# The second product of a fused attention and MLP kernel with its operands exchanged

## The chip, the cores and the metric

The kernel runs on one core of a Trainium2 chip. The metric is the device time in microseconds of one execution. TensorE multiplies matrices (its weight loads are listed as PEld), VectorE (DVE) and ScalarE (ACT) move and transform tiles, GpSimd (POOL) does elementwise work and issues DMAs, and SyncE (SP) issues DMAs.

## The reference

```python
B, N, m, C = 4, 12480, 32, 128          # x: (B, N, C), inducing: (m, C)

def mab(q, kv):                          # one attention head, no projections
    s = (q @ kv.transpose(0, 2, 1)) / sqrt(C)
    a = exp(s - s.max(-1)); a /= a.sum(-1) + 1e-09
    return a @ kv

h = mab(I, x)                            # 32 inducing points attend to the tokens
y = mab(x, h).reshape(B * N, C)          # the tokens attend to the 32 results

hid = y @ w_in                           # (49920, 128) @ (128, 2048)
g = maximum(hid, 0) + alpha * minimum(hid, 0)
out = g @ w_out                          # (49920, 2048) @ (2048, 128), float32
```

## The kernel before

A batch of 12480 tokens is 6 super-tiles of 2048 tokens (`SUP`) and a rest of 192. A super-tile is 4 groups of 512 tokens (`GRP`), so a batch has 25 groups: 24 of 512 tokens and one of 192.

The second attention is never formed by itself. Per super-tile, `b_scores` multiplies the tokens with `hT` (the 32 results of the first attention) and ScalarE takes the exponentials into `e2`, with 4 groups stacked in the 128 partitions, 32 each. SyncE writes `e2` to DRAM (L371) and `b_rep` reads it back into `rep` (L379), in which the 32 rows of a group stand four times. `b_den` sums the exponentials by a product with `pick`; the reciprocals `rd` are kept and applied at the very end, since everything in between is linear under a positive factor: alpha * h + (1 - alpha) * max(h, 0) splits the activation into a linear part (`linear`, with `hA`) and a ReLU part whose weight `W1` holds w_out times (1 - alpha).

The work of a group is cut into 4 fills (2 for the rest of 192 tokens), 392 fills in all. One fill is

- in `fill`: 4 products side by side in 4 row groups of 32 (`hW` stationary, `rep` moving, 512 columns), each into one of 6 rotating PSUM banks (`ring`), the 4 evacuated with ReLU to bfloat16 tiles `gt` by ScalarE (L448) or VectorE (L450);
- in `mm2`, one fill later: the second product, 16 matmuls of 128x128. A block of 128 tokens of `gt` is stationary and 128 columns of `W1` move. They add up in one of two PSUM tiles `accs`, with tokens in the partitions and channels in the columns.

When a group's last `mm2` is issued, it is put into `held`, and the next fill's `flush` calls `finish`: VectorE multiplies the 128x512 accumulator by the reciprocals into `ob` (L503), and GpSimd issues one store of 256 KB (L516) in rows of 2 KB. The last four stores go by SyncE, and the very last evacuation is shared by VectorE and ScalarE.

Which engine evacuates which bank, and where `flush` stands, comes from `make_plan`, a beam search over assumed costs of each fill; it is written out before the program is built. All other work (loads of the next batch from GpSimd's queue at L129, DMA transposes `xT` at L143 and `e1T` at L273 from SyncE's queue, scores, denominators) is put into slots of fills by `at(slot, task, j, cost)`. `pin` fixes the program order of each engine and each DMA queue to the order in the source. While a batch runs, the first attention of the next batch is computed in groups 0 to 17 or so; the last batch has no such work beside it.

Of the kernel before, what the change touches and what calls it, by code (L numbers as in the profile page):

```python
# [9 lines left out]
EXP = mybir.ActivationFunctionType.Exp  # L10
# [6 lines left out]
P = 128  # L17
# [8 lines left out]
def kernel(  # L26
# [30 lines left out]
    def pin(bi):  # L57
# [17 lines left out]
    xt_pool = ctx.enter_context(tc.tile_pool(name="xtp", bufs=2))  # L75
    gt_pool = ctx.enter_context(tc.tile_pool(name="gtp", bufs=4))
    head_pool = ctx.enter_context(tc.tile_pool(name="headp", bufs=3))
    rep_pool = ctx.enter_context(tc.tile_pool(name="repp", bufs=3))
    dram = ctx.enter_context(
        tc.tile_pool(name="e2d", bufs=3, space=bass.MemoryType.DRAM)  # L80
    )
    ob_pool = ctx.enter_context(tc.tile_pool(name="obp", bufs=3))
    psum = ctx.enter_context(
        tc.tile_pool(name="ps", bufs=1, space=bass.MemoryType.PSUM)
    )
    ring = [psum.tile([P, GRP], f32, name=f"ring{i}") for i in range(RING)]
    accs = [psum.tile([P, NB, C], f32, name=f"acc{i}") for i in range(2)]
    ring_n = [0]

    def bank():  # L90
# [4 lines left out]
    def mm(o, lhsT, rhs, start=True, stop=True, **kw):  # L95
        return pin(nc.tensor.matmul(o, lhsT, rhs, start=start, stop=stop, **kw))  # L96
# [5 lines left out]
    def new_batch(b):  # L102
        st = Batch()
        st.b = b
        st.xT = xt_pool.tile([C, NS, NQ, GRP], bf16, name="xT", tag="xT")
        st.xTr = xt_pool.tile([C, JR, PR], bf16, name="xTr", tag="xTr")
        st.xn = {}
        st.e1T = {}
        st.sc = scale
        st.rs = None  # L110
        st.e2 = {}
        st.d = {}
        st.rep = {}
        st.rden = {}
        if b > 0:
            st.es = work.tile([P, NS + 1], f32, name="es", tag="es")
            st.hacc = work.tile([P, C], f32, name="hacc", tag="hacc")
            nc.vector.memset(st.es[:], 0.0)
            nc.vector.memset(st.hacc[:], 0.0)
        return st  # L120
# [101 lines left out]
    def warm(st, n=1):  # L222
        for _ in range(n):
            mm(
                accs[0][:, 1:, :].rearrange("p k c -> p (k c)"), ident[:],
                st.xT[:, 0, 0, : 3 * P], start=False, stop=False, skip_group_check=True,
            )

# [123 lines left out]
        evac_h(st, st.hA[:], pa[:, :C])  # L352


    def b_scores(st, s):
        ps = bank()
        if s < NS:
            for q in range(NQ):
                mm(ps[32 * q : 32 * q + 32, :], st.hT, st.xT[:, s, q, :])
            e2 = work.tile([P, GRP], bf16, name="e2", tag="e2")  # L360
            pin(nc.scalar.activation(out=e2[:], in_=ps[:], func=EXP, scale=scale_of(st)))  # L361
            w = GRP
        else:
            mm(ps[0:M, :REM], st.hT, st.xTr[:].rearrange("c j p -> c (j p)"))
            e2 = work.tile([M, REM], bf16, name="e2r", tag="e2r")
            pin(nc.scalar.activation(out=e2[:], in_=ps[0:M, :REM], func=EXP, scale=scale_of(st, M)))
            w = REM

        nq = NQ if s < NS else 1
        st.d[s] = dram.tile([32 * nq, w], bf16, name="e2d", tag="e2d" if s < NS else "e2dr")  # L370
        pin(nc.sync.dma_start(out=st.d[s][:], in_=e2[:]))  # L371
        st.e2[s] = e2
# [11 lines left out]
    def b_scores_pe(st, q):  # L384
        if q == 0:
            st.rep0 = rep_pool.tile([P, NQ, GRP], bf16, name="rep", tag="rep")
        ps = bank()
        mm(ps[:], st.hT4[:], st.xT[:, 0, q, :])
        pin(nc.scalar.activation(
            out=st.rep0[:, q, :], in_=ps[:], func=EXP, scale=scale_of(st)  # L390
        ))
        st.rep[q] = st.rep0[:, q, :]

    def b_den(st, s):
        e2 = st.e2.pop(s)
        ps = bank()
        if s < NS:
            for j in range(NB):
                mm(ps[:, j * NQ : (j + 1) * NQ], e2[:, j * P : (j + 1) * P], pick[:])
            rd = work.tile([P, NB, NQ], f32, name="rd", tag="rd")  # L400
            pin(nc.vector.reciprocal(
                out=rd[:].rearrange("p j q -> p (j q)"), in_=ps[:, : NB * NQ]
            ))
        else:
            for j in range(JR):
                mm(ps[:PR, j : j + 1], e2[:, j * PR : (j + 1) * PR], pick[0:M, 0:1])
            rd = work.tile([PR, JR, 1], f32, name="rdr", tag="rdr")
            pin(nc.vector.reciprocal(
                out=rd[:].rearrange("p j q -> p (j q)"), in_=ps[:PR, :JR]
            ))  # L410
        st.rden[s] = rd

    def shape_of(g):
        return (P, NB, 1) if g < NS * NQ else (PR, JR, 2)

    held = []

    def flush():  # L420
        while held:
# [31 lines left out]

    def mm2(st, g, j, gt):
        pp, nb, cp = shape_of(g)
        acc = accs[(st.b * NG + g) % 2]
        begun = (g % 2 == 1 and st.b + g > 1) or cp > 1
        for r in range(4):
            for i in range(cp):
                c = r * NJ + j * cp + i  # L460
                for k in range(nb):
                    k0 = (i * nb + k) * pp
                    mm(
                        acc[:pp, k, :], gt[:, r, k0 : k0 + pp], W1[:, c, :],
                        start=(j == 0 and r == 0 and i == 0 and k == 0 and not begun),
                        stop=False, skip_group_check=True,
                    )
        if j == NJ // cp - 1 and st.b * NG + g > 0:
            held.append((st, g))

# [6 lines left out]
        return []  # L477

    def linear(st, groups):
        for k in range(NB):  # L480
            for r, g in enumerate(groups):
                pp, nb, cp = shape_of(g)
                if k < nb:
                    mm(
                        accs[(st.b * NG + g) % 2][:pp, k, :],
                        st.rep[g][32 * r : 32 * r + 32, k * pp : (k + 1) * pp],
                        st.hA[32 * r : 32 * r + 32, :],
                        start=((r == 1 or cp > 1) and k == 0), stop=False, skip_group_check=True,
                    )

    def finish(st, g):
        pp, nb, _ = shape_of(g)
        acc = accs[(st.b * NG + g) % 2]
        s, q = divmod(g, NQ)
        rd = st.rden[s]
        rq = rd[:, :, q : q + 1]
        final = (st.b, g) == (B - 1, NG - 1)
        cut = nb - 1 if final else nb
        rbc = bass.AP(
            tensor=rq.tensor, offset=rq.offset, ap=[rq.ap[0], [rq.ap[1][0], cut], [0, C]]  # L500
        )
        ob = ob_pool.tile([P, NB, C], f32, name="ob", tag="ob")
        pin(nc.vector.tensor_tensor(  # L503
            out=ob[:pp, :cut, :], in0=acc[:pp, :cut, :], in1=rbc, op=MULT
        ))
        if final:
            pin(nc.scalar.activation(  # L507
                out=ob[:pp, cut, :], in_=acc[:pp, cut, :], func=COPY, scale=rd[:pp, cut, 0:1]
            ))
        t0 = st.b * N + s * SUP  # L510
        if s < NS:
            dst = out[t0 : t0 + SUP, :].rearrange("(p q j) c -> q p j c", q=NQ, j=nb)[q]
        else:
            dst = out[t0 : t0 + REM, :].rearrange("(p j) c -> p j c", j=nb)
        ending = st.b == B - 1 and g >= NG - 4
        pin((nc.sync if ending else nc.gpsimd).dma_start(out=dst, in_=ob[:pp, :nb, :]))  # L516
        st.rep.pop(g)


# [93 lines left out]
    pin(nc.scalar.copy(out=xn0[:, 2:4, :], in_=xs[:, 2:4, :]))  # L613
    st.xn[0] = xn0

    pool = accs[0][:, 0, :M]
    den = accs[1][:, 0, 0:1]
# [43 lines left out]
    at(0, lambda: warm(st, 2), 0)  # L661
    at(0, lambda: b_scores_pe(st, 1), 1, (240, "A", 480))
    at(0, lambda: b_den(st, 0), 2, (130, "D", 250))
    at(1, w_amat, 2, (950, "D", 250))
    at(1, lambda: h_linear(st), 3, (80, "D", 250))
    at(2, late_finish, 0)
# [2 lines left out]
    for b in range(B):  # L669
        base = b * NG  # L670
        for s in range(1, NS + 1):
            g = base + s * NQ - 4
            at(g, lambda b=b, s=s: b_scores(states[b], s), 3, (320, "A", 490))
            at(g + 1, lambda b=b, s=s: b_rep(states[b], s), 3)
            at(g + 2, lambda b=b, s=s: b_den(states[b], s), 3, (130, "D", 250))
        if b + 1 < B:
            n = b + 1

# [16 lines left out]
            at(k + 2, lambda n=n: h_linear(states[n]), 3, (80, "D", 250))  # L695
            at(k + 3, lambda n=n: b_rep(states[n], 0), 0)
            at(k + 3, lambda n=n: b_den(states[n], 0), 1, (130, "D", 250))

# [76 lines left out]
    for b, g, j in fills:  # L775
        gt = fill(states[b], g, j)
        for fn, _ in tasks.pop((b * NG + g, j), []):
            fn()
        if prev is not None:
            mm2(*prev)  # L780
        prev = (states[b], g, j, gt)
    mm2(*prev)
    flush()
    assert not tasks, tasks


# [28 lines left out]
```

## Time and profile before

| What | Value |
|---|---|
| median of 3 runs | 592.72 us (592.19 to 592.80) |
| profiled execution, span from its first to its last instruction | 591.0 us |
| TensorE busy, weight loads busy | 578.7 us, 434.2 us |
| VectorE busy, ScalarE busy, GpSimd busy | 517.7 us, 502.5 us, 84.9 us |
| `mm2`: matmuls of 128x128 | 6272, mean record 220 ns |
| `fill`: matmuls with 512 columns | 1536, mean record 385 ns |
| evacuation of 128x512 by ScalarE, by VectorE | 875 x 602 ns, 661 x 687 ns |
| `ob` of 128x512 on VectorE | 96 x 681 ns |
| stores from GpSimd's queue, 256 KB each | 93, landing in 2.9 us (median) |

The profile gives the span as its only time of the profiled execution; the median of the runs is 1.7 us above it. "Busy" is the time in which an engine has an instruction in work. Matmuls are pipelined: their records overlap, so the number of them times the mean is more than the busy time. "A x16" in the chain or the timeline stands for 16 instructions of one kind in a row. DMA shares are a mean over the core's 16 DMA engines.

### The profile page before, as it was taken

To read this page: it belongs to the slowest core of one execution; us is meant where nothing else is said; L and a number is where in the kernel's file an instruction comes from. 1 tells how busy PE (TensorE), PEld (TensorE's weight loads), DVE (VectorE), ACT (ScalarE), POOL (GpSimd) and SP (SyncE) were. 2 spreads that over 40 slices of the span, in tenths; PEclk is the share of its full clock that TensorE was granted. 3 is DMA by queue.
4 is the path that set the end of the run, shared out by engine and by line. 5 is a ranking of instruction groups with operands and counts; after the bars stand their busy time and mean duration, and the time that the engine had idled before them with its cause. 6 is when DMAs were issued, how large, how long until landed. Compare 5 with 4: busy or idle time off the path is not lost.

```text
span 591.0 us, 21769 instructions
## 1 busy us (share of the span) xinstructions
PE 578.7 (98%) x9218; PEld 434.2 (73%) x9219; DVE 517.7 (88%) x869; ACT 502.5 (85%) x988; POOL 84.9 (14%) x170
## 2 busy tenths in 40 slices
PE   5999999999999999999999999999999999999997
PEld 4677777777777777777777777777777777777776
DVE  3688998999889989998989899988988998998996
ACT  2579888888889988888888998888888988989987
POOL 6631111101011111110111111101101101101100
PEclk9999999999999999999999999999999999999999
DMA  9973978751237569953126597985122221221211
GB/s 198 210 174 90 177 149 163 154 140 55 86 87 165 125 128 185 171 137 92 60 83 142 121 163 129 185 159 131 59 70 80 89 93 54 92 91 56 94 47 62
DMA packets 81825, 70.10 MB, mean 119 GB/s; under 512 B 55440, under 2 KB 71072, under 8 KB 81728
## 3 DMA queue, kind: packets, MB, share of 16 engines
q0 software_dynamic: 12528, 38.51, 26.0%
q1 hardware_dynamic: 69056, 29.68, 25.0%
q8 instruction: 72, 1.18, 0.8%
q10 hardware_dynamic: 144, 0.52, 0.2%
q14 instruction: 25, 0.20, 0.1%
HBM read 40.20 MB, written 28.75 MB: 117 GB/s over the span
## 4 chain that ended last, share of the span: by engine, by line
PE 97%; DVE 1%; DMA 1%; ACT 1%; issue 0%; SPq 0%
PE acc L96 68%; PE ring L96 27%; PE ring L172 1%; DMA ind_f<-in_inducing_dram 1%; ACT gt L448 0%; DVE xT L178 0%; DVE gt L450 0%; DVE ob L503 0%; DVE xn L612 0%; ACT xT L180 0%; SPq L526 0%; ACT ob L507 0%; DVE hT L246 0%; DVE ind_b L562 0%; PE ring L565 0%
## 5 line engine op out<-in xcount | busy, mean ns | idle before, releaser
L448 ACT ACTIVATE gt<-ring 128x512 bf16<-128x512 f32 x899 | 469.5, 599 | 67.8 <-ACT gt L448 27.4
L450 DVE TENSOR_SCALAR gt<-ring 128x512 bf16<-128x512 f32 x669 | 435.1, 685 | 52.2 <-PE ring L96 37.8
L96 PE MATMUL acc<-W,gt 128*128 128x128 bf16 x6272 | 417.9, 220 | 0.2 <-DVE ob L503 0.2
L96 PEld LDWEIGHTS <-gt 128*128 128x128 bf16 x6272 | 352.4, 98 | 79.6 <-issue 76.8
L96 PE MATMUL ring<-rep,hW 32*128 32x512 bf16 (+1 forms) x1600 | 157.3, 379 | 0.0
L516 POOL DMA_DIRECT2D out_dram<-ob x96 | 51.8, 540 | 476.5 <-DVE ob L503 412.6
L96 PEld LDWEIGHTS <-hW 32*128 32x128 bf16 x1600 | 41.1, 91 | 41.6 <-issue 0.5
L503 DVE TENSOR_TENSOR ob<-acc,rd 128x512 f32<-128x512 f32 x96 | 65.4, 681 | 2.5 <-PE acc L96 2.5
L96 PE MATMUL acc<-hA,rep 32*128 32x128 bf16 x392 | 19.8, 214 | 0.0
L96 PEld LDWEIGHTS <-rep 32*128 32x128 bf16 x392 | 15.6, 93 | 5.6
L129 POOL DMA_DIRECT2D xn<-in_x_dram x28 | 15.3, 551 | 3.3 <-DMA xn<-in_x_dram 2.4
L197 ACT ACTIVATE e1t<-ring 128x256 bf16<-128x256 f32 (+1 forms) x13 | 4.8, 371 | 10.5 <-PE ring L96 10.4
L178 DVE COPY xT<-ring 128x1024 bf16<-128x1024 bf16 (+1 forms) x12 | 8.0, 669 | 5.2 <-PE ring L172 4.8
L361 ACT ACTIVATE e<-ring 128x512 bf16<-128x512 f32 x18 | 11.0, 612 | 0.0
L269 ACT ACTIVATE e<-ring 128x512 bf16<-128x512 f32 x18 | 10.9, 605 | 0.0
L96 PE MATMUL ring<-xT,hT 128*32 128x512 bf16 (+1 forms) x97 | 10.0, 389 | 0.0
L172 PE MATMUL ring<-ident,xn 128*128 128x128 bf16 x96 | 8.8, 249 | 0.9 <-DVE xn L612 0.9
L172 PEld LDWEIGHTS <-xn 128*128 128x128 bf16 x96 | 6.8, 112 | 1.0 <-DVE xn L612 1.0
L96 PEld LDWEIGHTS <-hT 128*32 128x32 bf16 (+1 forms) x122 | 3.7, 92 | 5.1 <-issue 2.6
L96 PE MATMUL ring<-xn,e1T 128*32 128x128 bf16 x288 | 7.4, 221 | 0.0
L96 PE MATMUL ring<-xT,IT 128*32 128x512 bf16 x72 | 7.2, 390 | 0.0
L565 PE MATMUL ring<-ident,ind_b 32*128 32x32 bf16 x1 | 0.2, 205 | 6.1 <-DVE ind_b L562 6.1
(87 smaller groups left out, 113.6 us busy)
## 6 DMA issues: line engine op xcount, KB each, us to landing
out_dram<-ob POOLq DMA_DIRECT2D x93, 256.0 KB, 2.9
rep<-e2d SPq DMA_DIRECT2D x92, 128.0 KB, 3.4
xn<-in_x_dram POOLq DMA_DIRECT2D x18, 512.0 KB, 6.7
e2d<-e SPq DMA_DIRECT2D x24, 128.0 KB, 2.0
xn<-in_x_dram POOLq DMA_DIRECT2D x10, 256.0 KB, 8.5
w_out_f<-in_moe_w_out_dram POOLq DMA_DIRECT2D x4, 256.0 KB, 11.1
out_dram<-ob SPq DMA_DIRECT2D x3, 256.0 KB, 2.3
xs<-in_x_dram ACTq DMA_DIRECT2D x1, 512.0 KB, 4.9
```

The source lines that it names most:

```text
L96: return pin(nc.tensor.matmul(o, lhsT, rhs, start=start, stop=stop, **kw))
L129: pin(nc.gpsimd.dma_start(out=xn[:, i * w : (i + 1) * w, :], in_=src[:, i * w : (i + 1) * w, :]))
L172: pin(nc.tensor.transpose(tp[:, k * P : (k + 1) * P], xn[:, q, j * C : (j + 1) * C], ident[:]))
L178: pin(nc.vector.tensor_copy(out=dst, in_=tp[:, :w]))
L197: pin(nc.scalar.activation(out=e1t[:pp, :nb, :].rearrange("p k m -> p (k m)"), in_=ps[:pp, : nb * M], func=EXP, scale=scale,))
L269: pin(nc.scalar.activation(out=e1[:], in_=ps[:], func=EXP, scale=scale, accum_out=st.es[:, u : u + 1]))
L361: pin(nc.scalar.activation(out=e2[:], in_=ps[:], func=EXP, scale=scale_of(st)))
L448: pin(nc.scalar.activation(out=gt[:, r, :w], in_=ps[:, :w], func=RELU))
L450: pin(nc.vector.tensor_relu(gt[:, r, :w], ps[:, :w]))
L503: pin(nc.vector.tensor_tensor(out=ob[:pp, :cut, :], in0=acc[:pp, :cut, :], in1=rbc, op=MULT))
L516: pin((nc.sync if ending else nc.gpsimd).dma_start(out=dst, in_=ob[:pp, :nb, :]))
L565: nc.tensor.transpose(itp[:, :M], ind_b[:], ident[:M, :M])
```

## The change

The second product exchanges its operands. A 128x128 block of `W1` is now stationary and all 512 tokens of a `gt` tile move, so a fill has 4 matmuls in place of 16 and the accumulator has channels in the partitions and tokens in the columns. `linear` is exchanged in the same way.

The output must leave with tokens as rows. `finish` now has VectorE transpose the accumulator in blocks of 32x32 from PSUM into a new tile `ot`, and GpSimd multiply `ot` by the reciprocals into `ob`. After the block transposes, partition 32a + i of `ob` holds, for each block b of 32 tokens, channels 32a to 32a + 31 of its i-th token. So a group's output is stored in 4 DMAs, one for each a, of 512 pieces of 128 bytes. All of them are issued from SyncE's queue, held back in the list `late` for two more fills.

To let the pieces fall on the right tokens, the columns of `e2` and `rep` are put in another order (`tokens_of` on the moving operand of the scores, `turned` on the exponentials' reading of PSUM). The reciprocals must stand along the partitions in the same order, four times: `b_den` writes them to DRAM (`rt`), and a new task `b_turn`, one group later, reads them back in 4 DMAs as `rdT`. The plan's costs are unchanged.

```diff
+    def tokens_of(st, s, q):
+        return st.xT[:, s].rearrange("c j (q p) -> c j q p", q=NQ)[:, :, q, :]
+
+    def turned(ap, n):
+        return ap.rearrange("p (j i t) -> p t j i", j=n, i=32)
+
     def b_scores(st, s):
...
-                mm(ps[32 * q : 32 * q + 32, :], st.hT, st.xT[:, s, q, :])
+                mm(ps[32 * q : 32 * q + 32, :], st.hT, tokens_of(st, s, q))
...
+        pin(nc.scalar.activation(
+            out=e2[:].rearrange("p (t j i) -> p t j i", j=n, i=32),
+            in_=turned(ps[:pp, :w], n), func=EXP, scale=scale_of(st, pp),
+        ))
...
     def b_den(st, s):
...
+        rt = dram.tile([pp, n, nq], f32, name="rt", tag="rt" if s < NS else "rtr")
+        pin(nc.sync.dma_start(out=rt[:], in_=rd[:]))
+        st.rt[s] = rt
+
+    def b_turn(st, s):
+        n, nq, pp = (NB, NQ, P) if s < NS else (JR, 1, PR)
+        rdT = rd_pool.tile(
+            [P, pp // 32, n * nq], f32, name="rdT", tag="rdT" if s < NS else "rdTr"
+        )
+        src = st.rt.pop(s)[:].rearrange("(m i) k q -> i m (k q)", i=32)
+        for a in range(4):
+            pin(nc.sync.dma_start(out=rdT[32 * a : 32 * a + 32], in_=src))
+        st.rden[s] = rdT[:].rearrange("p m (k q) -> p k m q", q=nq)
...
+    late = []
+
+    def stores(end=False):
+        for x in list(late):
+            x[0] -= 1
+            if end or x[0] < 0:
+                late.remove(x)
+                for a in range(4):
+                    pin(nc.sync.dma_start(
+                        out=x[1][a], in_=x[2][32 * a : 32 * a + 32]
+                    ))
...
     def mm2(st, g, j, gt):
...
-                for k in range(nb):
-                    k0 = (i * nb + k) * pp
-                    mm(
-                        acc[:pp, k, :], gt[:, r, k0 : k0 + pp], W1[:, c, :],
-                        start=(j == 0 and r == 0 and i == 0 and k == 0 and not begun),
-                        stop=False, skip_group_check=True,
-                    )
+                mm(
+                    acc[:, :t], W1[:, c, :], gt[:, r, i * t : (i + 1) * t],
+                    start=(j == 0 and r == 0 and i == 0 and not begun),
+                    stop=False, skip_group_check=True,
+                )
...
     def linear(st, groups):
...
+            mm(
+                accs[(st.b * NG + g) % 2][:, :t], st.hA[32 * r : 32 * r + 32, :],
+                st.rep[g][32 * r : 32 * r + 32, :t],
+                start=(r == 1 or cp > 1), stop=False, skip_group_check=True,
+            )
 
     def finish(st, g):
...
-        ob = ob_pool.tile([P, NB, C], f32, name="ob", tag="ob")
-        pin(nc.vector.tensor_tensor(
-            out=ob[:pp, :cut, :], in0=acc[:pp, :cut, :], in1=rbc, op=MULT
+        ot = ot_pool.tile([P, GRP], f32, name="ot", tag="ot")
+        pin(nc.vector.transpose(out=ot[:, :t], in_=acc[:, :t]))
+        ob = ob_pool.tile([P, GRP], f32, name="ob", tag="ob")
+        pin(nc.gpsimd.tensor_tensor(
+            out=ob[:, :t].rearrange("p (k m c) -> p k m c", k=nb, c=32),
+            in0=ot[:, :t].rearrange("p (k m c) -> p k m c", k=nb, c=32),
+            in1=rbc, op=MULT,
         ))
-        if final:
-            pin(nc.scalar.activation(
-                out=ob[:pp, cut, :], in_=acc[:pp, cut, :], func=COPY, scale=rd[:pp, cut, 0:1]
-            ))
...
         if s < NS:
-            dst = out[t0 : t0 + SUP, :].rearrange("(p q j) c -> q p j c", q=NQ, j=nb)[q]
+            dst = out[t0 : t0 + SUP, :].rearrange(
+                "(i b q) (a k) -> q a i b k", b=t // 32, q=NQ, k=32)[q]
...
-        ending = st.b == B - 1 and g >= NG - 4
-        pin((nc.sync if ending else nc.gpsimd).dma_start(out=dst, in_=ob[:pp, :nb, :]))
+        late.append([2, dst, ob[:, :t].rearrange("p (b k) -> p b k", k=32)])
...
+    at(1, lambda: b_turn(st, 0), 0)
...
+            at(g + 3, lambda b=b, s=s: b_turn(states[b], s), 3 if s < NS else 1)
...
+            at(k + 4, lambda n=n: b_turn(states[n], 0), 0)
...
         if prev is not None:
             mm2(*prev)
+        stores()
         prev = (states[b], g, j, gt)
     mm2(*prev)
     flush()
+    stores(True)
```

More of the change, by code (lines that the diff above doesn't have):

```diff
@@ L77 @@
     head_pool = ctx.enter_context(tc.tile_pool(name="headp", bufs=3))
+    rd_pool = ctx.enter_context(tc.tile_pool(name="rdp", bufs=3))
     rep_pool = ctx.enter_context(tc.tile_pool(name="repp", bufs=3))
@@ L81 @@
     )
+    ot_pool = ctx.enter_context(tc.tile_pool(name="otp", bufs=2))
     ob_pool = ctx.enter_context(tc.tile_pool(name="obp", bufs=3))
@@ L86 @@
     ring = [psum.tile([P, GRP], f32, name=f"ring{i}") for i in range(RING)]
-    accs = [psum.tile([P, NB, C], f32, name=f"acc{i}") for i in range(2)]
+    accs = [psum.tile([P, GRP], f32, name=f"acc{i}") for i in range(2)]
     ring_n = [0]
@@ L114, in new_batch @@
         st.rden = {}
+        st.rt = {}
         if b > 0:
@@ L224, in warm @@
             mm(
-                accs[0][:, 1:, :].rearrange("p k c -> p (k c)"), ident[:],
+                accs[0][:, P:], ident[:],
                 st.xT[:, 0, 0, : 3 * P], start=False, stop=False, skip_group_check=True,
@@ L358, in b_scores @@
             for q in range(NQ):
-                mm(ps[32 * q : 32 * q + 32, :], st.hT, st.xT[:, s, q, :])
+                mm(ps[32 * q : 32 * q + 32, :], st.hT, tokens_of(st, s, q))
             e2 = work.tile([P, GRP], bf16, name="e2", tag="e2")
-            pin(nc.scalar.activation(out=e2[:], in_=ps[:], func=EXP, scale=scale_of(st)))
-            w = GRP
+            pp, w, n = P, GRP, NB
         else:
@@ L365, in b_scores @@
             e2 = work.tile([M, REM], bf16, name="e2r", tag="e2r")
-            pin(nc.scalar.activation(out=e2[:], in_=ps[0:M, :REM], func=EXP, scale=scale_of(st, M)))
-            w = REM
+            pp, w, n = M, REM, JR
+        pin(nc.scalar.activation(
+            out=e2[:].rearrange("p (t j i) -> p t j i", j=n, i=32),
+            in_=turned(ps[:pp, :w], n), func=EXP, scale=scale_of(st, pp),
+        ))
         nq = NQ if s < NS else 1
@@ L387, in b_scores_pe @@
         ps = bank()
-        mm(ps[:], st.hT4[:], st.xT[:, 0, q, :])
+        mm(ps[:], st.hT4[:], tokens_of(st, 0, q))
         pin(nc.scalar.activation(
-            out=st.rep0[:, q, :], in_=ps[:], func=EXP, scale=scale_of(st)
+            out=st.rep0[:, q, :].rearrange("p (t j i) -> p t j i", j=NB, i=32),
+            in_=turned(ps[:], NB), func=EXP, scale=scale_of(st),
         ))
@@ L396, in b_den @@
         ps = bank()
[L397 to L402, printed above, removed]
-            ))
[L404 to L411, printed above, removed]
+        n, nq, pp = (NB, NQ, P) if s < NS else (JR, 1, PR)
+        for k in range(n):
+            mm(
+                ps[:pp, k * nq : (k + 1) * nq], e2[:, k * pp : (k + 1) * pp],
+                pick[: 32 * nq, :nq],
+            )
+        rd = work.tile([pp, n, nq], f32, name="rd", tag="rd" if s < NS else "rdr")
+        pin(nc.vector.reciprocal(
+            out=rd[:].rearrange("p k q -> p (k q)"), in_=ps[:pp, : n * nq]
+        ))
[3 more added lines that the diff above has]
+    def b_turn(st, s):
+        n, nq, pp = (NB, NQ, P) if s < NS else (JR, 1, PR)
+        rdT = rd_pool.tile(
[5 more added lines that the diff above has]
+        st.rden[s] = rdT[:].rearrange("p m (k q) -> p k m q", q=nq)
     def shape_of(g):
@@ L418 @@
     held = []
+    late = []
[7 more added lines that the diff above has]
+                        out=x[1][a], in_=x[2][32 * a : 32 * a + 32]
+                    ))
     def flush():
@@ L455, in mm2 @@
         pp, nb, cp = shape_of(g)
+        t = pp * nb
         acc = accs[(st.b * NG + g) % 2]
@@ L479, in linear @@
     def linear(st, groups):
[L480 to L489, printed above, removed]
+        for r, g in enumerate(groups):
+            pp, nb, cp = shape_of(g)
+            t = pp * nb
+            mm(
+                accs[(st.b * NG + g) % 2][:, :t], st.hA[32 * r : 32 * r + 32, :],
+                st.rep[g][32 * r : 32 * r + 32, :t],
+                start=(r == 1 or cp > 1), stop=False, skip_group_check=True,
+            )
@@ L491, in finish @@
     def finish(st, g):
         pp, nb, _ = shape_of(g)
+        t = pp * nb
         acc = accs[(st.b * NG + g) % 2]
         s, q = divmod(g, NQ)
[L495 to L498, printed above, removed]
+        rq = st.rden[s][:, :, :, q : q + 1]
         rbc = bass.AP(
-            tensor=rq.tensor, offset=rq.offset, ap=[rq.ap[0], [rq.ap[1][0], cut], [0, C]]
+            tensor=rq.tensor, offset=rq.offset, ap=[rq.ap[0], rq.ap[1], rq.ap[2], [0, 32]]
@@ L501, in finish @@
         )
-        ob = ob_pool.tile([P, NB, C], f32, name="ob", tag="ob")
-        pin(nc.vector.tensor_tensor(
-            out=ob[:pp, :cut, :], in0=acc[:pp, :cut, :], in1=rbc, op=MULT
-        ))
-        if final:
-            pin(nc.scalar.activation(
-                out=ob[:pp, cut, :], in_=acc[:pp, cut, :], func=COPY, scale=rd[:pp, cut, 0:1]
-            ))
+        ot = ot_pool.tile([P, GRP], f32, name="ot", tag="ot")
+        pin(nc.vector.transpose(out=ot[:, :t], in_=acc[:, :t]))
+        ob = ob_pool.tile([P, GRP], f32, name="ob", tag="ob")
@@ L510, in finish @@
+        pin(nc.gpsimd.tensor_tensor(
+            out=ob[:, :t].rearrange("p (k m c) -> p k m c", k=nb, c=32),
+            in0=ot[:, :t].rearrange("p (k m c) -> p k m c", k=nb, c=32),
+            in1=rbc, op=MULT,
+        ))
         t0 = st.b * N + s * SUP
         if s < NS:
-            dst = out[t0 : t0 + SUP, :].rearrange("(p q j) c -> q p j c", q=NQ, j=nb)[q]
-        else:
-            dst = out[t0 : t0 + REM, :].rearrange("(p j) c -> p j c", j=nb)
-        ending = st.b == B - 1 and g >= NG - 4
@@ L516, in finish @@
-        pin((nc.sync if ending else nc.gpsimd).dma_start(out=dst, in_=ob[:pp, :nb, :]))
+            dst = out[t0 : t0 + SUP, :].rearrange(
+                "(i b q) (a k) -> q a i b k", b=t // 32, q=NQ, k=32)[q]
+        else:
+            dst = out[t0 : t0 + REM, :].rearrange("(i b) (a k) -> a i b k", b=t // 32, k=32)
+        late.append([2, dst, ob[:, :t].rearrange("p (b k) -> p b k", k=32)])
         st.rep.pop(g)
@@ L614 @@
     st.xn[0] = xn0
-    pool = accs[0][:, 0, :M]
-    den = accs[1][:, 0, 0:1]
+    pool = accs[0][:, :M]
+    den = accs[1][:, 0:1]
     halves = [(u, i) for u in order for i in range(1 if u == NS else 2)]
```

## The prediction

> **What bounds the kernel now.** I read the busy table first, then the chain of waits in order of time, then TensorE's timeline, and last the busy windows and the queues.
>
> ```profile
> PE 578.7 (98%) x9218; PEld 434.2 (73%) x9219; DVE 517.7 (88%) x869; ACT 502.5 (85%) x988; POOL 84.9 (14%) x170
> ```
>
> ```profile
> 201.29 1.00 PE acc L96 x16
> 202.29 0.33 PE ring L96 x4
> 202.62 1.00 PE acc L96 x16
> 203.62 0.33 PE ring L96 x4
> ```
>
> A busy TensorE proves little, but the chain does: it holds TensorE alone, fill after fill, 1.00 us for the 16 matmuls of `mm2` and 0.33 us for the 4 of `fill`, 1.33 us together, with no wait between them. TensorE waits for nobody; its instruction stream is the time. The timeline splits the 1.00 us:
>
> ```profile
> 205.21 1.07 PE L96 MATMUL acc<-W,gt 128*128 128x128 bf16 x16
> 206.21 0.40 PE L96 MATMUL ring<-rep,hW 32*128 32x512 bf16 x4
> ...
> 218.01 0.40 PE L96 MATMUL ring<-xT,hT 128*32 128x512 bf16 x4
> 218.23 0.40 PE L96 MATMUL ring<-xn,e1T 128*32 128x128 bf16 x16
> ```
>
> A matmul of 128 columns has a record of 0.22 us, so 16 lasting 1.07 are (1.07 - 0.22) / 15 = 0.0565 us apart. The last starts 0.85 after the first and the next kind at 1.00: 0.15, of which 0.0565 is its own pitch and 0.096 a hand-over between full-array and 32-row matmuls. The hand-over shows on the way back too (4 matmuls of 512 columns side by side take 0.33, not 0.22). The last two lines give the pitch at 512 columns with no such change: 218.01 to 218.23, 0.216 us in the records, at all six places where these two kinds meet. Granted clock 1.00 throughout.
>
> ```profile
> 40.00:580.00 540.00, 539.53 (x8550) 403.57 (x8549) 487.83 (x810) 475.71 (x935) 62.60 (x116) 1.00 0.50 115
> ```
>
> The columns are PE, weight loads, DVE, ACT, POOL, clock, DMA share and GB/s. Between 40 and 580 us VectorE is busy 90.3% and ScalarE 88.1%. So a faster TensorE has some 10% of room before the evacuations become the limit.
>
> **The change part by part.** *Second product.* The number of moved columns is the same: 16 x 128 = 4 x 512. The weight loads that go were hidden already (a 98 ns record, but a start every 0.0565 us beside the matmuls). What is saved is the fixed part of the pitch: 16 x 0.0565 = 0.904 becomes 4 x 0.216 = 0.864. The hand-over stays, since the array still changes between 128 and 32 rows: 1.00 becomes 0.96, and a fill goes from 1.326 to 1.286 us. Of the 392 fills 384 are of this kind: 384 x 0.040 = 15.4 us. The other 8 (192 tokens) go from 16 matmuls to 8 of 192 columns; at (0.216 - 0.0565) / 384 = 0.000415 us per column these take 0.083 each: 0.904 - 0.664 = 0.24, 1.9 us in all. `linear` goes from 8 matmuls in two row groups (4 x 0.0565 = 0.226) to 2 side by side (0.216): nothing. Sum -17.3 us, and all of it lies on the chain. Bounds: the records of 512 and 128 columns last 385 and 220 ns, 0.43 ns per column, which makes four matmuls 0.887 and the sum -9; a hand-over that vanished with the longer matmul would make it 384 x 0.136 = -52, but 512-column matmuls already show it after `fill`. I take -17, by the row with both starts.
>
> [...]
>
> *Output on VectorE.* 96 `TENSOR_TENSOR` of 128x512 (681 ns, 65.4 us in all) become 96 transposes of the same bank into the same kind of tile. No transpose on VectorE is in the trace. Nearest rows: this one and the cast of 128x512 f32 from PSUM (680 ns). No f32 read of that size from PSUM beats them here, so nothing is gained; above, two passes, one pitch of 0.60 more. I take 0.03 more. Cover: evacuations of two to three fills. Matching in the records each evacuation to the matmul that writes its bank again, the closest are 50 to 130 ns apart, and 40 ns per fill now come off that. So some of the gain returns as waits for a bank in the fill that holds the transpose: there VectorE has 0.60 + 2 x 0.60 = 1.8 us to do against 1.286, and must catch up in the other three. I allow 3 us (0 to 8). VectorE's share becomes 488 / 523 = 93%.
>
> *Scaling on GpSimd.*
>
> ```profile
> 26.00 2.48 DVE L450 TENSOR_SCALAR gt<-ring 128x512 bf16<-128x512 f32 x4 [0.18 <-PE ring L96]
> 23.94 4.06 POOL L590 TENSOR_TENSOR W<-w_out_f,om_al 128x512 bf16<-128x512 f32 x4 [3.85 <-DVE hT L246]
> ```
>
> A 128x512 multiply by a broadcast takes GpSimd 1.04 us. 96 are 100 us on an engine that is busy 85, less the 51.8 of store issues that leave. The four evacuations beside it keep their pace, (2.48 - 0.69) / 3 = 0.60: no slowing by GpSimd, cost 0. The x loads behind the multiply on POOL's queue have three groups (17 us) of lead.
>
> *Scores.* 24 exps read PSUM with a stride (612 ns now): from 0 to twice, at most 15 us of ScalarE's 12% idle; two in the prologue are on the path, +0.7 each at most. I take 0.
>
> *SyncE's queue.* Per four groups it now issues 4 `rep`, 1 `e2d`, and transposes. Added: 1 `rt` and 4 `rdT` (behind a landing, a group later; GpSimd waits for them, not TensorE), and 16 stores of 512 pieces. One issue takes 0.42 us:
>
> ```profile
> 198.75 1.20 SPq L273 DMA_TRANSPOSE e1T<-e  x1
> 199.99 2.49 SPq L143 DMA_TRANSPOSE xT<-xn  x1
> 202.59 2.65 SPq L379 DMA_DIRECT2D rep<-e2d  x4
> ```
>
> Issue times hardly depend on the pieces (`e2d` with 128 rows 0.34, with 32 rows 0.32), so in a stretch that loads the next batch two groups (11.4 us) need 3.7 for transposes, 2.0 for the old and turned small copies and 8 x 0.42 = 3.4 for stores: 9.1 us. It fits. What waits behind: `rep`, whose last issue ends 7.2 to 9 us ahead of its first matmul in these stretches and lands in 3 to 4, so 4 to 5 us are left; then `xT`, `e1T`.
>
> *The pieces themselves.* No 128-byte write is in the trace. Rows of 2048 bytes (the SyncE stores from 576 us) work out at 88 ns each, and the 384-byte copies here at 31:
>
> ```profile
> q1 hardware_dynamic: 240, 0.06, 6.4%
> ```
>
> (147.5 to 153 us: 0.064 x 16 engines x 5.5 us = 5.6 us for 160 pieces and 80 four-byte writes of 9 ns.) The line through both gives 22 ns at 128 bytes; the bounds are 9 and 31. Queue 1 then gets 2048 x 22 / 16 = 2.8 us per group. Over 20 to 130 us it holds 38.8%, which is 4.5 us in two groups; with 5.6 that is 10.1 of 11.4. I take no cost, with little to spare.
>
> [...]
>
> *The end.* Before, the last product is followed by 0.30 (VectorE), 0.36 (ScalarE) and one store. Now: transpose 0.35, multiply about 0.5, then eight stores of two groups at 0.42 on one queue: +2 us (1 to 3).
>
> Sum against the profiled execution: 591.0 - 17.3 + 3 + 2 = 578.7 us. The runs' median, 592.72, is 1.7 above its span: 580.4. I predict 580.5, own range 575 to 592.
>
> **The rivals.** *SyncE's queue falls behind (slower).* It decides where the pieces fill queue 1: 4096 x t / 16 = 11.4 - 4.5, t = 27 ns. Each batch but the last has some 80 us of such loading. At 31 ns the queue is 9% over: 7 us late after a stretch, 5 of it slack, three times 2 us: 587. At 40 ns 29%: 23 late, three times 18 us: 635. Past 32 ns it is slower than before. For it: DMA share 0.84 from 60 to 120 us already. Against: the 9 ns that the smallest writes take. 0.20, time 594 to 660.
>
> *The transpose takes two passes (slower).* 92 in the window x 0.6 adds 55 us to 488: VectorE needs 543 where TensorE needs 523, so VectorE is the bound: 592.7 + 3 + 2 + up to 10 for its own waits, 597 to 607. It decides at some 0.9 us per transpose. 0.12.
>
> *Nothing comes of it.* The pitch of 512 columns is the slow bound (-9) and waits and end take it back: 592. 0.06. Other slow causes 0.04.
>
> **How the numbers follow.** The forecast has 0.58. A measurement here tells 0.2% (1.2 us). Faster 0.58, same 0.06, slower 0.36. The range 575 to 612 takes in the forecast, the nothing case, the two-pass transpose and the lower part of the late queue; some 0.15 lies above and 0.03 below.
>
> **What would show it.** Right: `acc` x4 with 0.96 us in the chain and 1.29 per fill; transposes near 0.71 us; VectorE at 93%; `rep` landing before its matmul. Wrong: a chain with DMA or `rep` in it, SyncE issues over 1 us each in the loading stretches, GpSimd waiting for `ob` buffers, VectorE in the chain, or `acc` x4 still at 1.00.

## The result, and the profile after

The changed kernel takes 623.51 us (619.77 to 626.61, 4 runs) against 592.76 us before (592.19 to 594.34): 1.0516 times as long, interval 1.0481 to 1.0551. The profiled execution took 619.77 us with a span of 618.0 us.

First the page: busy times, the granted clock in 40 slices, queue 1 (SyncE's: packets, MB, share of the time of 16 engines), and the shares of the chain that ended last; behind it the last line as it was before.

```profile
PE 568.0 (92%) x4185; PEld 198.8 (32%) x4255; DVE 517.7 (84%) x869; ACT 503.8 (82%) x987; POOL 137.9 (22%) x174
PEclk9999989799999999999999998999999999999998
q1 hardware_dynamic: 294112, 55.39, 47.6%
PE 79%; DMA 13%; SPq 2%; issue 2%; ACT 1%; DVE 1%; POOLq 0%; POOL 0%; DVEq 0%
```

```profile
PE 97%; DVE 1%; DMA 1%; ACT 1%; issue 0%; SPq 0%
```

TensorE has less to do than before (568.0 us, a part of it at a lower clock) and now idles 8% of the span. VectorE and ScalarE are as busy in us as before, a smaller share of the longer span; GpSimd has 137.9 us in place of 84.9 and is far from full. The chain, 97% TensorE before, is now 79% TensorE and 13% DMA, and the clock line, all nines before, has a 7 and some 8s in the loop. The chain of waits in order of time shows one such place (start, duration, what):

```profile
100.42 0.33 PE ring L98 x4
100.75 0.97 PE acc L98 x4
101.71 0.20 PE ring L98
...
102.19 7.36 DMA xT<-xn
...
109.60 0.62 PE ring L98 x4
110.22 1.82 PE acc L98 x4
112.04 0.55 PE ring L98 x4
112.58 1.82 PE acc L98 x4
```

Up to 101.7 the product runs nearly as forecast, 0.97 and 0.33 us. There the chain leaves TensorE for `xT`, the transposed tokens of the next batch: they land at 109.55, and TensorE, which had work until 105.3, is idle for 4.3 us. After that the same four matmuls take 1.82 us: for 6.8 us the granted clock is 0.5. Why `xT` came so late stands in the timeline of SyncE's queue (start, duration of the issues, what):

```profile
86.42 2.62 SPq L146 DMA_TRANSPOSE xT<-xn  x1
89.15 2.45 SPq L390 DMA_DIRECT2D rep<-e2d  x4
91.69 3.00 SPq L445 DMA_DIRECT2D out_dram<-ob  x4
94.79 3.25 SPq L420 DMA_DIRECT2D rt<-rd  x1
98.15 2.59 SPq L445 DMA_DIRECT2D out_dram<-ob  x4
100.83 1.25 SPq L276 DMA_TRANSPOSE e1T<-e  x1
102.19 2.15 SPq L146 DMA_TRANSPOSE xT<-xn  x1
```

The queue doesn't rest here: each row begins 0.1 us after the one above it ends. From one `xT` to the next, which is two groups of work, it needs 15.8 us, and TensorE needs 11.2 for two groups where nothing is late (a version below shows it). The eight stores take 5.6 of them, and `rt`, one small copy right behind stores, 3.25 (0.31 to 0.37 where it is quickest). This goes on through every stretch that prepares the next batch: SyncE issues for 17.3 to 18.6 of each 20 us from 40 to 140 us, where the kernel before had 3.6 to 12.5. All twelve pauses of TensorE over 0.5 us end with `xT` or `xTr` (its counterpart for a batch's rest). It is not that their landing got slower: `xT` lands 4.4 us after its issue has begun (median), against 6.5 before. Nor did they wait for their x: each of the 21 was issued 0.10 to 0.13 us after the row ahead of it on the queue had ended.

In the records the loop, from the first product of `fill` to the end of the last matmul, grew from 562.2 to 585.0 us, and the end behind it from 3.3 to 7.5. The loop holds 14 pauses between matmuls with 24.5 us in all beyond the usual pitch, and 20.5 us at clock 0.5, which cost at most half of that (some of it lies in the pauses).

### The profile page after: what moved, and what is told of

It reads as the page before. It is cut to its first block, busy times and chain, and to the rows that moved or that the text cites. A ratio compares the mean times of both kernels' runs of the same rounds, so it can differ in the third digit from the quotient of the medians.

```text
span 618.0 us, 12607 instructions
## 1 busy us (share of the span) xinstructions
PE 568.0 (92%) x4185; PEld 198.8 (32%) x4255; DVE 517.7 (84%) x869; ACT 503.8 (82%) x987; POOL 137.9 (22%) x174
## 4 chain that ended last, share of the span: by engine, by line
PE 79%; DMA 13%; SPq 2%; issue 2%; ACT 1%; DVE 1%; POOLq 0%; POOL 0%; DVEq 0%
PE acc L98 55%; PE ring L98 23%; DMA xT<-xn 6%; DMA rep<-e2d 3%; DMA xTr<-xnr 3%; DMA out_dram<-ob 1%; SPq L445 1%; PE ring L175 1%; ACT gt L477 1%; DMA ind_f<-in_inducing_dram 1%; SPq L390 1%; SPq L276 0%; DVE xT L181 0%; DVE gt L479 0%; SPq L420 0%
## 5 line engine op out<-in xcount | busy, mean ns | idle before, releaser
L98 PE MATMUL acc<-gt,W 128*128 128x512 bf16 x1530 | 397.1, 381 | 9.9 <-issue 8.7
L529 POOL TENSOR_TENSOR ob<-ot,rdT 128x512 f32<-128x512 f32 (+1 forms) x100 | 105.0, 1050 | 463.4 <-DVE ot L527 349.7
L98 PEld LDWEIGHTS <-W 128*128 128x128 bf16 x1600 | 125.7, 98 | 175.6 <-issue 84.5
L98 PE MATMUL ring<-rep,hW 32*128 32x512 bf16 (+1 forms) x1600 | 162.4, 382 | 0.8 <-DMA rep<-e2d 0.4
L527 DVE STREAM_TRANSPOSE ot<-acc 128x512 f32<-128x512 f32 (+1 forms) x100 | 69.3, 693 | 3.8 <-PE acc L98 3.8
L98 PE MATMUL acc<-rep,hA 32*128 32x512 bf16 (+1 forms) x100 | 19.4, 369 | 0.0
L98 PEld LDWEIGHTS <-IT 128*32 128x32 bf16 x75 | 2.1, 93 | 28.7 <-DMA xT<-xn 16.6
```

Source lines behind the costliest of these rows:

```text
L527: pin(nc.vector.transpose(out=ot[:, :t], in_=acc[:, :t]))
L529: pin(nc.gpsimd.tensor_tensor(out=ob[:, :t].rearrange("p (k m c) -> p k m c", k=nb, c=32), in0=ot[:, :t].rearrange("p (k m c) -> p k m c", ...
```

## The experiments

Theory A: SyncE's queue, which works in order (each row above begins 0.1 us after the one ahead of it has ended), is the bound; it has more to issue in a loading stretch than there is time, because of the four stores per group. The rivals: the 128-byte pieces fill the DMA engines, whoever issues them (the mechanism by which the prediction priced its rival); the new work on VectorE and GpSimd delays TensorE; and the exchanged product brings less than forecast by itself.

**Stores from GpSimd.**

```diff
                 for a in range(4):
-                    pin(nc.sync.dma_start(
+                    pin(nc.gpsimd.dma_start(
                         out=x[1][a], in_=x[2][32 * a : 32 * a + 32]
...
```

> The changed kernel with its 400 stores (4 per group, 512 pieces of 128 bytes each) issued from GpSimd's queue in place of SyncE's; nothing else differs. Theory A (SyncE's queue is the bound: 400 issues of 0.68 us are 271 us of it, it is busy 18 of 20 us while the next batch is loaded, and the DMA transposes and rep come late): SyncE loses those 271 us, the 24.5 us of TensorE gaps before the scores and rep go, and with them the halved clock; 580 us, 575 to 588, if GpSimd issues 512 pieces in about 1 us. Theory B (the DMA engines or the memory are slowed by the 128-byte pieces): the pieces are the same, so still over 610 us. Theory C (the product, transposes and GpSimd's multiply themselves cost it): also over 610 us.

Measured: 586.55 us against 592.51, ratio 0.9901 (0.9886 to 0.9916). The same stores from another queue turn 5% slower into 1% faster. The busy windows of 60 to 120 us tell queue and DMA engines apart; first the changed kernel, then this one (last columns: granted clock, DMA share, GB/s):

```profile
60.00:120.00 60.00, 51.61 (x343) 16.16 (x347) 45.07 (x75) 43.89 (x88) 10.69 (x12) 0.91 0.78 140
```

```profile
60.00:120.00 60.00, 59.69 (x439) 19.43 (x437) 55.72 (x93) 53.50 (x108) 40.79 (x58) 1.00 1.01 166
```

The slow kernel uses its DMA engines less (0.78) than the fast one (1.01; packets overlap, up to 31 of one store in a run below, and the share passes 1). Full DMA engines were not what made it slow. This run changes more than the queue, though: in the records a store by GpSimd shows as 32 packets and not as 512. The run of one store led by 128, below, keeps both the pieces and the queue. What this version leaves is an end of 8.8 us.

**The same number of stores from SyncE, in rows of 2 KB.** The output then lies elsewhere.

```diff
-                "(i b q) (a k) -> q a i b k", b=t // 32, q=NQ, k=32)[q]
+                "(q a i b) (e k) -> q a i (b e) k", q=NQ, a=4, b=4, k=32)[q]
```

> The changed kernel with the same 4 stores per group from SyncE, but each of 32 rows of 2 KB in place of 512 pieces of 128 bytes (for the groups of 512 tokens; the output then lies in other places than the reference's). Theory A, where the issue time grows with the pieces: an issue falls from 0.62 to 0.34 to 0.42 us, SyncE loses about 100 to 120 us, gaps before the scores mostly go: 580 to 592 us. If the number of issues is what counts, not their pieces: still 0.6 us each and over 610 us. Theory B: 580 to 590 us as well, as the pieces are gone; theory C: over 610 us.

Measured: 584.11 us, ratio 0.9858 (0.9843 to 0.9873). Its SyncE timeline at the same place:

```profile
81.09 2.96 SPq L146 DMA_TRANSPOSE xT<-xn  x1
84.15 1.95 SPq L390 DMA_DIRECT2D rep<-e2d  x4
86.19 1.77 SPq L445 DMA_DIRECT2D out_dram<-ob  x4
88.38 0.34 SPq L420 DMA_DIRECT2D rt<-rd  x1
88.82 1.90 SPq L445 DMA_DIRECT2D out_dram<-ob  x4
90.82 1.33 SPq L276 DMA_TRANSPOSE e1T<-e  x1
92.25 2.97 SPq L146 DMA_TRANSPOSE xT<-xn  x1
```

The same list from `xT` to `xT` now takes 11.2 us, TensorE's own pace. Eight stores cost 3.7 us in place of 5.6, an issue 0.42 in place of 0.62 (medians), and `rt` behind them is back at 0.34. So the price of the pieces is paid on the queue, in two places: the store's own issue, and the item behind a run of stores.

**One store of 2048 pieces in place of four of 512.**

```diff
-                for a in range(4):
-                    pin(nc.sync.dma_start(
-                        out=x[1][a], in_=x[2][32 * a : 32 * a + 32]
-                    ))
+                pin(nc.sync.dma_start(out=x[1], in_=x[2]))
```

> The changed kernel with one store per group from SyncE of 2048 pieces of 128 bytes, in place of four of 512. Theory A with a cost per issue (0.34 us and 0.5 ns per piece, by the line through e2d's 128 and the store's 512 pieces): one issue of about 1.4 us in place of 4 x 0.62, SyncE loses some 110 us, 580 to 595 us. Theory A with a cost per piece alone (0.645 us per 512, 1.26 ns each): one issue takes 2.5 us, SyncE is as late as before, 615 to 625 us. Theory B: 615 to 625 us, as the pieces are the same.

Measured: 874.86 us, ratio 1.4766 (1.4738 to 1.4793), far from every expectation. The timeline:

```profile
68.78 0.56 SPq L444 DMA_DIRECT2D out_dram<-ob  x1
69.45 6.49 SPq L276 DMA_TRANSPOSE e1T<-e  x1
...
82.06 0.58 SPq L444 DMA_DIRECT2D out_dram<-ob  x1
82.75 5.70 SPq L420 DMA_DIRECT2D rt<-rd  x1
```

The store itself is issued in 0.56 us, but what stands behind it mostly takes 4 us or more to issue (89 of 97 times, median 5.8). In the records the 2048 packets of one store run for some 6.4 us, which is the delay seen, and never more than 8 of them overlap. At the 12.0 ns that a packet of 128 bytes lasts in the changed kernel, 2048 are 24.6 us, which in 6.4 us makes 3.8 at a time: an estimate from these two numbers, and near the 4 engines that the expectation of the next run but one reads from this run. The author's guess was that the store's leading dimension on the DRAM side, `a`, of size 4, sets this number. The next run but one tests that.

**The kernel before with the changed kernel's stores.** Its own output layout, cut into 4 x 512 pieces of 128 bytes from SyncE, two fills late.

```diff
+                for a in range(4):
+                    pin(nc.sync.dma_start(
+                        out=x[1][:, :, 32 * a : 32 * a + 32],
+                        in_=x[2][:, :, 32 * a : 32 * a + 32],
+                    ))
...
-        ending = st.b == B - 1 and g >= NG - 4
-        pin((nc.sync if ending else nc.gpsimd).dma_start(out=dst, in_=ob[:pp, :nb, :]))
+        late.append([2, dst, ob[:pp, :nb, :]])
...
```

> The kernel before (first and last products as they were, VectorE's multiply, no turned reciprocals), with only its output stores changed: 4 per group from SyncE, held back two fills, 512 pieces of 128 bytes each. Theory A: SyncE's queue gets 400 issues of 0.6 us more (150 us become 400), comes late while batches are loaded, and the kernel loses 5 to 20 us and 2 to 4 at its end: 600 to 617 us. Theory B: the same range. Theory C (product, transposes, GpSimd): nothing but the end changes, 592 to 597 us.

Measured: 614.58 us, ratio 1.0397 (1.0358 to 1.0436). The stores alone, with no product exchanged, no transpose and no turned reciprocals, cost 22 us. This clears the new work; queue and pieces, for which the same range was expected, it doesn't tell apart. In its profile 15.2 us are pauses. The longest, 7.1, is TensorE waiting for VectorE, and that for an `ob` buffer whose store landed 14.4 us after its issue. From 50 to 60 us the DMA share is 1.02 there, most of it the x loads from GpSimd's queue, and eight stores took 19.7 us to issue. So at this place it may be the DMA engines, and not the number of issues, that held the stores up; no run tests it. The changed kernel has a share of 0.73 from 40 to 60 us. Of the other pauses the long ones are `xT` again.

**One store of 2048 pieces, led by a dimension of 128.** A group writes its 32 channels of all 2048 tokens of the super-tile; the output lies elsewhere.

```diff
+                if len(x[1].shape) == 3:
+                    pin(nc.sync.dma_start(out=x[1], in_=x[2]))
+                    continue
...
-                "(i b q) (a k) -> q a i b k", b=t // 32, q=NQ, k=32)[q]
+                "(p r) (q k) -> q p r k", r=16, q=NQ)[q]
```

> The changed kernel with one SyncE store per group in place of four, again of 2048 pieces of 128 bytes, but with the DRAM side led by a dimension of 128 in place of 4 (a group then writes its 32 channels of all 2048 tokens of the super-tile, so that the output lies elsewhere). Theory A with the reading of the other one-store kernel that it used 4 of 16 DMA engines: all 16 are used here, a store takes 2048 x 12 ns / 16 = 1.5 us to move, SyncE has 100 issues in place of 400, and the time is 582 to 588, no gap over 1 us before scores or rep. Rival (it was the number of pieces in one DMA that made what follows on the queue wait, 2048 x 11.7 ns at one place): again some 5 to 6 us behind each store, 850 to 880. Rival B (SyncE pays per piece written, whatever the number of stores): 2048 pieces cost 4 x 0.62 = 2.5 us as before, 610 to 626.

Measured: 589.73 us, ratio 0.9949 (0.993 to 0.9969); somewhat above the range expected by theory A and far from both rivals. The same pieces in the same number of stores as in the last run but one, 285 us faster: the leading dimension, with the layout that goes with it, made that loss. The 2048 packets of a store now run for 1.4 us (median) in place of 6.4, and up to 31 of them overlap in place of 8. (They last 13.1 ns in the mean here; the 11.7 of the expectation is in no trace.) By the same estimate that is 19 at a time (2048 x 13.1 ns in 1.4 us) against 3.8; the packet records name no engine, so the 4 and the 16 of the expectation are not shown. Against the changed kernel the pieces and the queue are the same with a quarter of the issues, and the pauses fall from 24.5 to 4.0 us. Not all is gone, since the item behind a store still waits at times:

```profile
89.73 0.57 SPq L445 DMA_DIRECT2D out_dram<-ob  x1
90.41 4.99 SPq L420 DMA_DIRECT2D rt<-rd  x1
```

**Two stores from SyncE, two from GpSimd.**

```diff
-                    pin(nc.sync.dma_start(
+                    pin((nc.sync, nc.gpsimd)[a % 2].dma_start(
```

> The changed kernel with two of a group's four stores from SyncE and two from GpSimd, everything else the same. Theory A (the queue falls behind only where SyncE has more to issue than time, in the stretches with the next batch): 200 x 0.62 = 124 us leave SyncE, its busy time in the loading stretches falls from 17 to 18.6 of 20 us to some 13 to 15, no gap over 1 us is left, and the loop is 550 to 552; the end has 6 stores on each queue, 5 to 6 us; 582 to 585. Rival (the cost is proportional to SyncE's stores, through the load on the DMA engines or on TensorE's operands): half of the 34 us of gaps and halved clock, 600 to 606.

Measured: 585.62 us, ratio 0.989 (0.9872 to 0.9908). Half of the stores gone from SyncE brings nearly all of the gain, as for a queue that fits or doesn't, and not half of it. Two numbers missed: the loop is 554.3 us with one pause of 1.2, and SyncE's busy time did not fall everywhere; in the middle of a loading stretch (80 to 120 us) it is still 18.6 to 18.7 of 20 us, and 13.5 to 14.9 on both sides of it. The issues of `xT` take 3.2 us in the median here. The kernel before has 3.1, so it is the changed kernel's 1.9 that is short. The records show with what it goes: here `xT` took 1.3 to 1.9 us to issue where the DMA share was below 0.7 meanwhile, and 2.2 to 5.8 where it was 0.95 or more. Whether the one causes the other was not tested. So here the queue's busy time didn't tell how late it was: 18.6 of 20 us at most in the changed kernel too.

**Eight stores of 256 pieces.**

```diff
-                for a in range(4):
+                n = x[2].shape[1] // 2
+                for a in range(8):
+                    i, h = a // 2, a % 2 * n
                     pin(nc.sync.dma_start(
-                        out=x[1][a], in_=x[2][32 * a : 32 * a + 32]
+                        out=x[1][i][:, h : h + n],
+                        in_=x[2][32 * i : 32 * i + 32, h : h + n],
...
```

> The changed kernel with each of its four SyncE stores cut in two: eight stores of 256 pieces, the same bytes, the same pieces, the same queue. Theory A (SyncE pays mainly per store issued): an issue takes 0.45 to 0.6 us, which is 400 more of them and some 150 to 200 us more on SyncE's queue; in the stretches with the next batch two groups need some 3 to 4 us more of it, about 9 pairs in each of 3 batches: 650 to 720. Rival (SyncE or the DMA engines pay per piece, the number of stores doesn't matter): an issue takes 0.3 us and the time stays at 618 to 630.

Measured: 717.08 us, ratio 1.2113 (1.2076 to 1.215), at the upper end of theory A and outside the rival's. An issue takes 0.45 us; SyncE's issues add up to 597 us in place of 496, 101 more where 150 to 200 were expected, and the kernel is 94 us longer: here, with the queue already full, a us more on it cost nearly a us of the kernel. The DMA share from 60 to 120 us is only 0.70.

**The exchanged product alone.** The kernel before with only `mm2` and `linear` exchanged; stores, VectorE's multiply and the rest as before, so the output's layout and scaling are left out.

```diff
-                for k in range(nb):
-                    k0 = (i * nb + k) * pp
-                    mm(
-                        acc[:pp, k, :], gt[:, r, k0 : k0 + pp], W1[:, c, :],
...
+                t = pp * nb
+                mm(
+                    acc[:].rearrange("p k c -> p (k c)")[:, :t],
+                    W1[:, c, :], gt[:, r, i * t : (i + 1) * t],
...
```

> The kernel before with only mm2 and linear exchanged: no transposes, no multiply on GpSimd, stores as before; the accumulator, which now has channels in its partitions, is multiplied and stored as if it held tokens there, so the output's layout and scaling are left out. It measures the product by itself. Forecast of the prediction: -17.3 us, 575.5. Reading of the changed kernel's trace (the loop of the version with stores from GpSimd is 11.6 us shorter): 580.5 to 581.5 if the transposes, the multiply and the reciprocals' turn cost TensorE nothing; if they cost some of the gain, this kernel is faster than 580 by that much, down to 575.5.

Measured: 580.50 us, ratio 0.9799 (0.9782 to 0.9815), so -12.0 us. Its chain:

```profile
200.16 0.97 PE acc L96 x4
201.12 0.33 PE ring L96 x4
201.45 0.97 PE acc L96 x4
```

Its loop is 549.9 us; with transposes, GpSimd's multiply and the turned reciprocals beside it, but the stores off SyncE, 550.8. All that work costs TensorE 1 us.

**A shorter end, two versions.** Both have the stores from GpSimd. In the first the last four groups' stores go from SyncE at once, and those left at the very end from SyncE and ScalarE in turn:

```diff
-                    pin(nc.sync.dma_start(
+                    eng = (nc.sync, nc.scalar)[a % 2] if end else x[3]
+                    pin(eng.dma_start(
...
-        late.append([2, dst, ob[:, :t].rearrange("p (b k) -> p b k", k=32)])
+        ending = st.b == B - 1 and g >= NG - 4
+        late.append([0 if ending else 2, dst, ob[:, :t].rearrange("p (b k) -> p b k", k=32),
+                     nc.sync if ending else nc.gpsimd])
```

> The changed kernel with its stores from GpSimd, and its last four groups' stores from SyncE without the delay of two fills, the very last ones shared by SyncE and ScalarE. Theory A (SyncE's in-order queue was the only thing wrong with the change, and what GpSimd's stores leave is an end of 9.1 us against 3.6 before): the end falls to 4 to 5.5 us, the loop stays at 550 to 551, sum 581.5 to 584, and it beats the kernel before by 1.5 to 2%. Rival B (the end's stores hide something that must be waited for anyway, the multiply on GpSimd or the landing of the pieces): the end stays at 8 us or more, 585.5 to 587.

Measured: 585.81 us, ratio 0.9898 (0.9872 to 0.9924); a miss. Ten of the last twelve stores stood in one queue again, behind `rdT`, which waits for `rt`:

```profile
575.87 1.93 SPq L430 DMA_DIRECT2D rdT<-rt  x4
577.90 6.79 SPq L446 DMA_DIRECT2D out_dram<-ob  x10
```

The end fell only to 7.5 us, and the profiled execution also had a pause of 1.2 us for a `rep` that took 7.8 us to land. The second keeps all but the last two groups' stores on GpSimd and gives 4 of those to each of SyncE and ScalarE:

```diff
-                    pin(nc.sync.dma_start(
+                    eng = (nc.sync, nc.scalar)[a % 2] if x[3] else nc.gpsimd
+                    pin(eng.dma_start(
...
-        late.append([2, dst, ob[:, :t].rearrange("p (b k) -> p b k", k=32)])
+        last = st.b == B - 1 and g >= NG - 2
+        late.append([9 if last else 1 if st.b == B - 1 and g == NG - 3 else 2, dst,
+                     ob[:, :t].rearrange("p (b k) -> p b k", k=32), last])
```

> The changed kernel with its stores from GpSimd; only the last two groups' stores, 8 in all, wait for the end and go from SyncE and ScalarE in turn, 4 on each, and the last but two leaves GpSimd one fill earlier. Theory A: the loop 550.5 to 554 as in the other versions with GpSimd's stores, and the end 5 to 6.5 us in place of 9.1 (the last multiply ends 1.5 us after the last product, then 4 issues of 0.65 on each queue, half of them ahead of that): 582.5 to 586. Rival (the end is set by something else than the number of issues on one queue): the end stays at 7.5 us or more, 585.5 to 588.

Measured: 583.69 us, ratio 0.9844 (0.9829 to 0.9858), the fastest of the versions that keep the output's layout: 1.6% under the kernel before, 6.4% under the changed one. The end is 5.5 us:

```profile
576.16 3.49 SPq L446 DMA_DIRECT2D out_dram<-ob  x4
576.16 2.72 ACTq L446 DMA_DIRECT2D out_dram<-ob  x4
```

All versions together; loop and end are of the profiled execution, SyncE is the sum of all its DMA issues:

| Version | stores | SyncE us | loop us | end us | median us |
|---|---|---|---|---|---|
| before | GpSimd, 1 per group | 156 | 562.2 | 3.3 | 592.7 |
| changed | SyncE, 4 x 512 pieces | 496 | 585.0 | 7.5 | 623.5 |
| from GpSimd | GpSimd, 4 x 512 | 230 | 550.8 | 8.8 | 586.6 |
| long rows | SyncE, 4 x 32 rows | 393 | 550.6 | 6.7 | 584.1 |
| one store, led by 4 | SyncE, 2048 | 761 | 821.2 | 28.4 | 874.9 |
| one store, led by 128 | SyncE, 2048 | 343 | 557.3 | 5.9 | 589.7 |
| half and half | SyncE and GpSimd, 2 x 512 each | 376 | 554.3 | 6.2 | 585.6 |
| eight stores | SyncE, 8 x 256 | 597 | 671.7 | 16.9 | 717.1 |
| before, its stores so cut | SyncE, 4 x 512 | 413 | 579.4 | 5.8 | 614.6 |
| product alone | as before | 154 | 549.9 | 3.4 | 580.5 |
| GpSimd, first short end | GpSimd, last four groups elsewhere | 237 | 554.0 | 7.5 | 585.8 |
| GpSimd, second short end | GpSimd, last two groups elsewhere | 229 | 550.9 | 5.5 | 583.7 |

## Why the prediction was wrong, step by step

**The step that failed is SyncE's queue: "9.1 us. It fits."** For two groups in a loading stretch it put 3.7 us for transposes, 2.0 for the small copies and 8 x 0.42 = 3.4 for stores. The rows above have 3.9 for `xT` and `e1T`, 2.45 and 3.25 for `rep` and `rt`, and 5.6 for the stores: 15.2, and 15.8 with the 0.1 between rows. Two terms were too small. A store was priced at the 0.42 of a `rep` copy, though it is another shape (0.62, or 0.70 with the gap to the next): +2.2 us. And the small copies were priced alone, not as they stand behind 2048 pieces: `rt` 3.25 in place of 0.34, +2.9. The other 1.0 us is longer issues of `rep` and the transposes. With either of the two alone the sum would have been near 11.3 to 12.0, over the edge or on it, so the slack of 2.3 us was gone with one of them. The prediction's own row could have told: four `rep` issues in 2.65 us are 0.66 each, and 0.42 is the median over the whole kernel. At 0.66 for the stores alone the sum is 11.0 of 11.4 us, and 12.0 with `rep` and `rdT` at that price too. The sentence it rested on, that issue times hardly depend on the pieces, is half right: from 32 to 2048 pieces an issue varied only between 0.42 and 0.62. But 0.2 us more on each of eight stores, with the gaps, used up 2.2 of the 2.3 us.

**The rival had the right queue and the wrong price.** "SyncE's queue falls behind", 594 to 660 us, held the time. But it was to be decided by the time of a piece, from 27 ns on. The 128-byte packets of the trace last 12.0 ns in the mean, where 22 was taken (9 to 31), so by that test the rival was out of reach while its result came true. The DMA engines were not full (a share of 0.78 from 60 to 120 us); the queue was. And past the full point the loss is not the lateness only: 24.5 us of pauses, some 10 from the lowered clock, 4.2 at the end. With these the sum is 592.7 - 12.0 + 1.0 + 24.5 + 10 + 4.2 = 620.4 us; the profiled execution took 619.8.

**Sizes.** The product: -17.3 forecast, -12.0 measured alone. The chain has 0.97 us for four matmuls, where 0.96 was put; the first of the three pitches is 0.226 and not 0.216 us, and the hand-over after the last is the 0.096 forecast (0.312 to the next kind). A fill takes 1.297 in place of 1.286, which makes 0.029 us of gain per fill where 0.040 was put; over 384 fills that is 4 of the 5.3 us missed. The rest is not followed up. The allowance of 3 us for bank waits was too much: 1 us. The end, put at +2, is +4.2, since twelve stores and not eight stood on the one queue:

```profile
607.21 8.57 SPq L445 DMA_DIRECT2D out_dram<-ob  x12
```

With the stores off SyncE and the end spread, the forecast's terms with the sizes measured account for the time: 592.7 - 12.0 + 1.0 + 2.2 = 583.9, measured 583.7. That this lies within the forecast's own range of 575 to 592 doesn't make the forecast right: it was made for stores on SyncE's queue.

**Right.** The transpose on VectorE (the 128x512 form lasts 707 ns; 0.71 was put, and the two passes did not happen), GpSimd's multiply (1.07 us against 1.04) with no slowing of the evacuations beside it (128x512 in 602 ns by ScalarE and 687 by VectorE, as before), the scores' strided exponentials at nothing (612 ns, as before):

```profile
L529 POOL TENSOR_TENSOR ob<-ot,rdT 128x512 f32<-128x512 f32 (+1 forms) x100 | 105.0, 1050 | 463.4 <-DVE ot L527 349.7
L527 DVE STREAM_TRANSPOSE ot<-acc 128x512 f32<-128x512 f32 (+1 forms) x100 | 69.3, 693 | 3.8 <-PE acc L98 3.8
```

GpSimd did wait for `ob` buffers (83.9 us in all, 16 times, for stores), one of the signs named for a wrong forecast, and the next batch's loads behind it on its queue went out later too (two of them at 91.8 and 103.3 us, against 86.9 and 98.4 with the stores from GpSimd), though no transpose was found waiting for one.

## What to carry to other kernels

Add up an in-order DMA queue row by row over the busiest stretch, with the duration that each shape of transfer has there and with what the next row pays behind a run of many small pieces; if the sum comes near the time that there is, as 9.1 of 11.4 us did here, treat the queue as the bound and put the new transfers on another queue. The queue that overflowed here took what stood behind it along, the transposes of the next batch, with which all twelve pauses of TensorE over 0.5 us ended, although every compute engine had room (TensorE 92% busy, VectorE 84%) and the DMA engines were less busy (0.78) than in the version from GpSimd (1.01). Once it fitted, taking more off it brought little: the loop is 554.3 us with half of the stores on SyncE and 550.8 with none.

## What the runs showed of the hardware

Some pauses of TensorE cost more than themselves. In the changed kernel four of the twelve pauses that left it idle for over 0.5 us (3.3, 4.3, 2.0 and 3.8 us) came with 3.4 to 6.8 us at half the granted clock, begun within the pause or up to 0.2 us behind it (behind the pause of 4.3 the four `acc` matmuls took 1.82 us in place of 0.97); a pause of 2.8 us did not, and in the first short-end version one of 1.2 us was followed by 3.4 us of it. So the length alone didn't decide it.

A store with 2048 pieces is issued in 0.54 to 0.57 us (medians), but the next DMA of another kind on the queue at times took 4 us or more to issue: with a leading dimension of 4 it did so 89 of 97 times, with 128 only 11 of 97.

In the changed kernel the 128-byte packets of the stores on SyncE's queue lasted 12.0 ns in the mean (199,680 of them), the queue's four-byte packets 9.8 ns.
